# One projection unit per block with two products in the row tiles, q kept per block, and FFN units in the last head of a one-core attention kernel

## The chip, the core and the metric

The kernel runs on one core of one Trainium2 chip. The metric is the time of one execution in microseconds of device time. A profiled execution has a span a little under that time (1976.3 us against 1978.3 us before). Engines are called as in the profile: PE is TensorE's matmul side, PEld its weight loads, DVE VectorE, ACT ScalarE, POOL GpSimd, SP SyncE.

## The reference

Layer norm, then 32 heads of attention of 2048 queries on 2048 cached keys with head dimension 192, gated by the silu of a SwiGLU FFN of the same normed input:

```python
def reference(A_x, A_k_cache, A_v_cache, A_wq, A_wo, B_x, B_w1, B_w3, B_w2):
    xn = _layernorm(A_x)                                  # [1, 2048, 640]
    q = heads(xn @ A_wq)                                  # 32 heads of 192
    p = softmax(q @ k_cache^T * 192 ** -0.5)
    s = concat(p @ v_cache) @ A_wo
    h = silu(xn @ B_w1) * (xn @ B_w3)                     # F = 1536
    g = silu(h @ B_w2)
    return A_x + s * g
```

## The kernel before

Work goes in blocks: one head and 512 queries. A block has 8 units. A unit is six score matmuls, one exp on ACT of a 128x1024 tile in PSUM (the memory that matmuls write their sums to), and sixteen value matmuls that add into two PSUM tiles, called the output banks here (`obank`; each takes two of PSUM's eight banks). Scores run two units ahead of the values. Each matmul uses 64 of the 128 rows of the array, and a neighbour uses the other 64 at the same time (row tiles).

In the loop of head h, the q of head h+1 is projected as well. The two row tiles take the two halves of one contraction, so their results must be added: ACT copies one, DVE adds the other. A block of q needs this twice (`half` 1 and 0), and each time takes one of the two PSUM buffers `st2` that the scores also rotate through. The weight columns beside the last 64 of q carry a strip of the FFN (gate in even heads, up in odd heads).

```python
ps_st = ...tile_pool(name="ps_st", bufs=2, space=PSUM)      # [P, 1024] f32: two banks each

def project(h, qb, half):                                   # cut: head 0 has its own form
    qAB, qC = qtiles[h]
    qs = slice(qb * 512, (qb + 1) * 512)
    dst, w = qAB[:, half, qs], (L["wqB"] if half else L["wq"])
    ps = ps_st.tile([P, 1024], F32, tag="st2", name="ps")
    for c in range(DC):                                     # 5
        for r in range(2):
            rows = slice(r * 64, (r + 1) * 64)
            nc.tensor.matmul(ps[:, r * 512:(r + 1) * 512], lhsT=w[rows, c, 0:P],
                             rhs=xnT[rows, c, qs], start=(c == 0), stop=(c == DC - 1))   # L319
    part = hbp.tile([P, 512], F32, tag="part", name="part")
    nc.scalar.copy(out=part[:], in_=ps[:, 0:512])                                        # L322
    nc.vector.tensor_tensor(out=dst, in0=ps[:, 512:1024], in1=part[:], op=ALU.add)       # L323
    # then DMA copies of 64-row halves of qAB into qC

# values(n), when a block ends: the two output banks are evicted side by side
    nc.scalar.copy(out=osum[:], in_=ov[0])                                               # L405
    nc.vector.tensor_copy(out=opart[:], in_=ov[1])                                       # L406
    nc.vector.tensor_tensor(out=osum[:], in0=osum[:], in1=opart[:], op=ALU.add)          # L407

for n, (h, qb, p) in enumerate(stream):
    scores(n + 2)
    if h + 1 < H and p == (5 if h == 0 else 0):
        project(h + 1, qb, 1)
    if h + 1 < H and p == (NPAIR - 1 if h == 0 else NPAIR // 2):
        project(h + 1, qb, 0)
    values(n)
    if p == 0 and n > 0:
        finish_block(n - 1)
    if p == (6 if h == 0 else 2) and h < 2 * NPIG:
        swiglu(h, qb)                 # even heads: tanh on ACT, then DVE
    # cut: head 0's own projections, layer norm, loads
```

After the last head follow the FFN units that are left (`ps_gu`, full-row matmuls), the FFN's second product (`ps_f`) and the output product (`ps_s`).

## Time and profile before

| | before |
|---|---|
| median time | 1978.34 us (4 runs, 1977.82 to 1978.42) |
| span of the profile | 1976.3 us |
| PE / ACT / DVE busy | 1952.1 / 1319.6 / 738.3 us |
| a steady block (heads 1 to 30), mean | 12.81 us |

The first part of the profile's page (busy time and share of the span) and its part on the chain of work that ended last:

```profile
PE 1952.1 (99%) x27311; PEld 1386.0 (70%) x27311; DVE 738.3 (37%) x1109; ACT 1319.6 (67%) x1525; POOL 333.2 (17%) x570
...
PE 96%; ACT 2%; DVE 1%; DMA 1%; issue 0%; ACTq 0%
```

PE is the limit, and the page hides something. Matmuls are pipelined and their ends are modelled, so a PE that is 99% busy can still pause. The Trainium skill warns of this busy time too ("Trainium Kernel Development and Optimization", section "Performance Expectations": matmul busy time is a bad metric for how close a kernel is to its limit, because matmuls are pipelined). So I read distances from the start of one group of matmuls to the start of the next. In this trace six scores take 0.647 us, sixteen values 0.665 us, ten projection matmuls 1.076 us; these are the floors. Units of a block, from first score matmul to the next unit's first score matmul, mean over heads 1 to 30, computed from the starts in the trace:

| unit of the block | 0 | 1 | 2 | 3 | 4 | 5 | 6 | 7 | block |
|---|---|---|---|---|---|---|---|---|---|
| before, us | 1.314 | 1.324 | 2.432 | 1.314 | 1.314 | 1.314 | 2.483 | 1.314 | 12.81 |

Six units are within 0.012 us of their floor (0.647 + 0.665 = 1.312). Units 2 and 6 hold a half projection; 0.647 + 0.665 + 1.076 would be 2.388, so they lose 0.044 and 0.095 us. In even heads the second loss is larger. Lines of the timeline in an even head (start, duration, engine, line, operation; in brackets the engine's idle time and what ended it):

```profile
804.97 0.62 ACT L345 ACTIVATE pt<-qAB 64x512 bf16<-64x512 bf16 x1
...
805.49 1.00 ACT L369 ACTIVATE pT<-st 128x1024 bf16<-128x1024 f32 x1
...
806.19 0.38 PE L366 MATMUL st<-qC,KC 64*128 64x512 bf16 x1
...
806.21 0.38 PE L367 MATMUL st<-qC,KC 64*128 64x512 bf16 x1
806.55 1.26 PE L319 MATMUL ps<-xnT,wq 64*128 64x512 bf16 x10
...
806.68 1.02 ACT L369 ACTIVATE pT<-st 128x1024 bf16<-128x1024 f32 x1 [0.18 <-PE st L367]
```

The last pair of scores starts at 806.19 and would be followed after 0.215 us. The projection starts only at 806.55, 60 ns after the exp of L369 ends (805.49 + 1.00): it needs the PSUM buffer that this exp reads, and tanh (L345) had delayed the exp. The pause is 0.145 us here; in odd heads, which have no tanh, it is 0.038 us (both are the medians too).

The opening of a block in the last head, where no projection stands between the end of a block and the next values:

```profile
1643.11 0.96 DVE L406 COPY opart<-obank 128x772 f32<-128x772 f32 x1 [7.23 <-PE obank L395]
...
1643.33 0.38 PE L367 MATMUL st<-qC,KC 64*128 64x512 bf16 x1
1643.40 0.80 ACT L405 COPY osum<-obank 128x772 f32<-128x772 f32 x1
1644.09 1.04 ACT L369 ACTIVATE pT<-st 128x1024 bf16<-128x1024 f32 x1
1644.23 0.96 DVE L407 TENSOR_TENSOR osum<-osum,opart 128x772 f32<-128x772 f32 x1 [0.17 <-ACT osum L405]
1644.25 0.84 PE L395 MATMUL obank<-vt,pT 64*128 64x193 bf16 x16 [0.55 <-ACT osum L405]
```

PE waits 0.73 us with the values (to 1644.25, instead of 1643.52) until both output banks have been read.

### The profile page before, as it was taken

How to read it: one execution, taken by the hardware profiler on the slowest of the kernel's cores; microseconds unless marked ns; L12 is line 12 of the kernel's file. 1: busy time of each engine (PE TensorE's matmuls, PEld its weight loads, DVE VectorE, ACT ScalarE, POOL GpSimd, SP SyncE). 2: the span in 40 equal slices, each digit the busy share in tenths (PEclk: the TensorE clock that was granted, in tenths of full speed). 3: DMA queues.
4: the chain of work that ended last, by engine and by line, in shares of the span. 5: the costliest groups of instructions: out<-in, count | busy, mean ns of one | idle time of the engine just before them, and what ended most of it. 6: DMA issues, size and time to landing. Idle time of an engine off the chain costs nothing.

```text
span 1976.3 us, 60169 instructions
## 1 busy us (share of the span) xinstructions
PE 1952.1 (99%) x27311; PEld 1386.0 (70%) x27311; DVE 738.3 (37%) x1109; ACT 1319.6 (67%) x1525; POOL 333.2 (17%) x570
## 2 busy tenths in 40 slices
PE   7999999999999999999999999999999999999998
PEld 5677777777777777777777777777777776577776
DVE  5433434333344443334333333443433333521111
ACT  4677787777777777777777777777778777210000
POOL 2222112112221221122122112212211210000000
PEclk9999999999999999999999999999999999999999
DMA  6223233334333434363334343433323230928883
GB/s 153 56 56 91 62 100 66 95 67 100 69 98 69 101 69 99 69 167 67 100 69 101 67 101 69 87 80 73 91 58 92 62 80 4 263 37 150 151 143 70
DMA packets 359718, 177.96 MB, mean 90 GB/s; under 512 B 305552, under 2 KB 346256, under 8 KB 359456
## 3 DMA queue, kind: packets, MB, share of 16 engines
q1 hardware_dynamic: 331824, 113.92, 27.4%
q0 software_dynamic: 23120, 56.72, 11.6%
q8 instruction: 215, 3.52, 0.8%
q10 hardware_dynamic: 4512, 3.41, 0.6%
q14 instruction: 47, 0.39, 0.1%
HBM read 55.44 MB, written 27.79 MB: 42 GB/s over the span
## 4 chain that ended last, share of the span: by engine, by line
PE 96%; ACT 2%; DVE 1%; DMA 1%; issue 0%; ACTq 0%
PE obank L395 34%; PE st L366 30%; PE ps L319 14%; PE ps_s L106 11%; PE st L367 3%; PE ps_f L560 3%; PE ps_gu L531 1%; PE ps_gu L534 1%; ACT pT L369 1%; DMA vt<-in_A_k_cache_dram 1%; PE ps L312 0%; DVE stats L275 0%; ACT osum L405 0%; PE pst L291 0%; ACT xnT L294 0%
## 5 line engine op out<-in xcount | busy, mean ns | idle before, releaser
L369 ACT ACTIVATE pT<-st 128x1024 bf16<-128x1024 f32 x1024 | 1048.9, 1024 | 347.4 <-PE st L367 347.3
L395 PEld LDWEIGHTS <-pT 64*128 64x128 bf16 x16384 | 745.6, 94 | 215.0 <-issue 7.7
L395 PE MATMUL obank<-vt,pT 64*128 64x193 bf16 x16384 | 867.1, 243 | 5.2 <-ACT osum L405 2.9
L366 PE MATMUL st<-qAB,KA 64*128 64x512 bf16 x1024 | 385.1, 376 | 1.6 <-ACT pT L369 0.9
L366 PE MATMUL st<-qC,KC 64*128 64x512 bf16 x1024 | 385.0, 376 | 0.8 <-DVE KC L244 0.8
L366 PE MATMUL st<-qC,KB 64*128 64x512 bf16 x1024 | 385.0, 376 | 0.2 <-ACT qC L329 0.2
L367 PE MATMUL st<-qAB,KA 64*128 64x512 bf16 x1024 | 385.1, 376 | 0.0
L367 PE MATMUL st<-qC,KC 64*128 64x512 bf16 x1024 | 385.0, 376 | 0.0
L367 PE MATMUL st<-qAB,KB 64*128 64x512 bf16 x1024 | 385.0, 376 | 0.0
L332 POOL DMA_DIRECT2D qC<-qAB x254 | 134.4, 529 | 1250.3 <-DVE rl_all L413 654.8
L323 DVE TENSOR_TENSOR qAB<-ps,part 128x512 bf16<-128x512 f32 x248 | 171.4, 691 | 421.8 <-ACT part L322 420.9
L406 DVE COPY opart<-obank 128x772 f32<-128x772 f32 x128 | 123.0, 961 | 425.4 <-PE obank L395 425.4
L106 PE MATMUL ps_s<-wo_sb,oT 128*128 128x256 bf16 (+3 forms) x1536 | 208.8, 299 | 0.0
L106 PEld LDWEIGHTS <-oT 128*128 128x128 bf16 x1536 | 148.4, 98 | 60.4
L366 PEld LDWEIGHTS <-KC 64*128 64x128 bf16 x1024 | 96.2, 94 | 105.1 <-DVE KC L244 1.1
L319 PE MATMUL ps<-xnT,wq 64*128 64x512 bf16 x1240 | 155.7, 376 | 0.3
L319 PE MATMUL ps<-xnT,wqB 64*128 64x512 bf16 x1240 | 155.7, 376 | 0.2 <-ACT pT L369 0.2
L322 ACT COPY part<-ps 128x512 f32<-128x512 f32 x248 | 147.7, 596 | 10.7 <-PE ps L319 0.9
L407 DVE TENSOR_TENSOR osum<-osum,opart 128x772 f32<-128x772 f32 x128 | 123.2, 963 | 21.3 <-ACT osum L405 20.8
L414 DVE TENSOR_TENSOR ostage<-osum,rl_all 128x768 bf16<-128x768 f32 x128 | 122.6, 958 | 4.4
L319 PEld LDWEIGHTS <-wq 64*128 64x128 bf16 x1240 | 67.2, 94 | 77.6 <-issue 26.4
L319 PEld LDWEIGHTS <-wqB 64*128 64x128 bf16 x1240 | 67.2, 94 | 71.4 <-issue 20.0
(75 smaller groups left out, 1263.3 us busy)
## 6 DMA issues: line engine op xcount, KB each, us to landing
vt<-in_A_v_cache_dram SPq DMA_DIRECT2D x32, 768.0 KB, 6.6
o_scr<-ostage SPq DMA_DIRECT2D x16, 1536.0 KB, 8.9
qC<-qAB POOLq DMA_DIRECT2D x381, 64.0 KB, 1.9
wq<-in_A_wq_dram POOLq DMA_DIRECT2D x32, 240.0 KB, 3.5
wo_sb<-in_A_wo_dram POOLq DMA_DIRECT2D x1, 7680.0 KB, 38.5
KC<-KA POOLq DMA_DIRECT2D x31, 128.0 KB, 4.8
KC<-KB POOLq DMA_DIRECT2D x31, 128.0 KB, 5.9
x_all<-in_A_x_dram SPq DMA_DIRECT2D x4, 640.0 KB, 9.3
```

Of the source, the lines that this page charges most:

```text
L106: nc.tensor.matmul(ps[:, 0:w], lhsT=oT[:, k, :], rhs=wo_sb[:, k, c0:c1], start=(k == 0), stop=(k == OC - 1))
L319: nc.tensor.matmul(ps[:, r * 512:(r + 1) * 512], lhsT=w[rows, c, 0:P], rhs=xnT[rows, c, qs], start=(c == 0), stop=(c == DC - 1))
L322: nc.scalar.copy(out=part[:], in_=ps[:, 0:512])
L323: nc.vector.tensor_tensor(out=dst, in0=ps[:, 512:1024], in1=part[:], op=ALU.add)
L332: nc.gpsimd.dma_start(out=qC[0:64, half, qs], in_=qAB[64:P, half, qs])
L366: nc.tensor.matmul(st2[:, 0:512], lhsT=k0, rhs=q0, start=r == 0, stop=r == 2)
L367: nc.tensor.matmul(st2[:, 512:1024], lhsT=k1, rhs=q1, start=r == 0, stop=r == 2)
L369: nc.scalar.activation(out=pT2[:], in_=st2[:], func=ACT.Exp, scale=att_scale)
L395: nc.tensor.matmul(obanks[r][:, j * 256:j * 256 + DH + 1], lhsT=pT2[r * 64:(r + 1) * 64, t * 512 + j * P:t * 512 + (j + 1) * P], rhs=vt[r ...
L406: nc.vector.tensor_copy(out=opart[:], in_=ov[1])
L407: nc.vector.tensor_tensor(out=osum[:], in0=osum[:], in1=opart[:], op=ALU.add)
L414: nc.vector.tensor_tensor(out=ostage[:, qb * 4:qb * 4 + 4, hg * DH:(hg + 1) * DH], in0=osum[:, :, 0:DH], in1=rl.unsqueeze(2).to_broadcast( ...
```

## The change

Its intent: one PSUM buffer and one opening per block for the projection instead of two; no adding of halves, so less for ACT and DVE; and work for PE to cover the eviction of the output banks in the last head too. A second copy of xn^T with its 64-row halves swapped (`xnS`) lets each row tile run through the whole contraction of a product of its own: row tile 0 makes the first 128 columns of q, row tile 1 the FFN strip and the last 64. DVE casts one result, ACT the other. The output banks are now added without a copy in between.

```diff
-    qp = att.enter_context(tc.tile_pool(name="qp", bufs=2))        # q of a whole head
-    pp = att.enter_context(tc.tile_pool(name="pp", bufs=6))
+    qp = att.enter_context(tc.tile_pool(name="qp", bufs=5))        # q of a block
+    pp = att.enter_context(tc.tile_pool(name="pp", bufs=4))
+    xnS = xsp.tile([P, DC, SQ], BF16, name="xnS")
 ... (the weights of both products in one tile W, 64 rows each; loads)
+            nc.sync.dma_start(out=xnS[0:64, :, qs], in_=xnT[64:P, :, qs])
+            nc.sync.dma_start(out=xnS[64:P, :, qs], in_=xnT[0:64, :, qs])
 ... (project(h, qb, half) goes, except for head 0)
+    def two_products(W, qs):
+        ps = ps_st.tile([P, 1024], F32, tag="st2", name="ps")
+        for j in range(2 * DC):
+            for r in range(2):
+                rows = slice(r * 64, (r + 1) * 64)
+                xs = xnT if j % 2 == r else xnS
+                nc.tensor.matmul(ps[:, r * 512:(r + 1) * 512], lhsT=W[rows, j, :], rhs=xs[rows, j // 2, qs],
+                                 start=(j == 0), stop=(j == 2 * DC - 1))
+        return ps
+    def cast_pair(qAB, ps):
+        nc.vector.tensor_copy(out=qAB[:, 0, :], in_=ps[:, 0:512])
+        nc.scalar.copy(out=qAB[:, 1, :], in_=ps[:, 512:1024])
 ... (project(h, qb) = two_products, cast_pair, copies to qC; ffn_open / ffn_close: the same with
 ...  128 gate and 128 up columns, then tanh and the products)
-        opart = osp.tile([P, 4, DH + 1], F32, tag="opart", name="opart")
         nc.scalar.copy(out=osum[:], in_=ov[0])
-        nc.vector.tensor_copy(out=opart[:], in_=ov[1])
-        nc.vector.tensor_tensor(out=osum[:], in0=osum[:], in1=opart[:], op=ALU.add)
+        nc.vector.tensor_tensor(out=osum[:], in0=osum[:], in1=ov[1], op=ALU.add)
     for n, (h, qb, p) in enumerate(stream):
+        if p == 0 and n > 0:
+            if h + 1 < H:
+                project(h + 1, qb)
+            else:
+                ffn_open(qb)
         scores(n + 2)
-        if h + 1 < H and p == (5 if h == 0 else 0):
-            project(h + 1, qb, 1)
-        if h + 1 < H and p == (NPAIR - 1 if h == 0 else NPAIR // 2):
-            project(h + 1, qb, 0)
+        if h == 0 and qb == 0 and p == 5:
+            project(1, 0)
         values(n)
 ...
+        if p == 4 and h + 1 == H:
+            ffn_close(qb)
 ... (the tail makes three quarters of its ps_gu units)
```

More of the change, by code (lines that the diff above doesn't have):

```diff
@@ L162, in _kernel_impl @@
     FL = F - FPIG
+    FL2 = FL - P
+    assert FL2 > 0
     x2 = A_x[0]
@@ L180, in _kernel_impl @@
     fw = main.enter_context(tc.tile_pool(name="fw", bufs=1))
-    WX = max(NQT * D, FC * D + 2 * DC * FL)
+    WX = max(NQT * D, FC * D + 2 * DC * FL2)
     att = ExitStack()
@@ L185, in _kernel_impl @@
     vtp = att.enter_context(tc.tile_pool(name="vtp", bufs=1))
+    xsp = att.enter_context(tc.tile_pool(name="xsp", bufs=1))
     wqp = att.enter_context(tc.tile_pool(name="wqp", bufs=2))
-    qp = att.enter_context(tc.tile_pool(name="qp", bufs=2))
-    qlp = att.enter_context(tc.tile_pool(name="qlp", bufs=2))
-    pp = att.enter_context(tc.tile_pool(name="pp", bufs=6))
+    qp = att.enter_context(tc.tile_pool(name="qp", bufs=5))
+    qlp = att.enter_context(tc.tile_pool(name="qlp", bufs=5))
+    pp = att.enter_context(tc.tile_pool(name="pp", bufs=4))
     stp = att.enter_context(tc.tile_pool(name="stp", bufs=1))
@@ L205, in load_x, with gate_cols, load_w0, load_wf @@
                           in_=x2[g * 512:(g + 1) * 512, :].rearrange("(t p) d -> p t d", p=P))
+    def gate_cols(h):
+        wsel = B_w1 if h % 2 == 0 else B_w3
+        return wsel[:, (h // 2) * PGW:(h // 2 + 1) * PGW]
+    def load_w0():
+        W = wqp.tile([P, 2 * DC, P], BF16, tag="W", name="W")
+        nc.gpsimd.dma_start(out=W[:, 0:DC, :], in_=A_wq[:, 0:P].rearrange("(c p) d -> p c d", p=P))
+        nc.gpsimd.dma_start(out=W[:, DC:2 * DC, 0:PGW], in_=gate_cols(0).rearrange("(c p) f -> p c f", p=P))
+        nc.gpsimd.dma_start(out=W[:, DC:2 * DC, PGW:P], in_=A_wq[:, P:DH].rearrange("(c p) d -> p c d", p=P))
+        loads.setdefault(0, {}).update(W=W)
     def load_w(h):
-        wq = wqp.tile([P, DC, DH], BF16, tag="wq", name="wq")
-        nc.gpsimd.dma_start(out=wq[:], in_=A_wq[:, h * DH:(h + 1) * DH].rearrange("(c p) d -> p c d", p=P))
-        wqB = wqp.tile([P, DC, P], BF16, tag="wqB", name="wqB")
+        W = wqp.tile([P, 2 * DC, P], BF16, tag="W", name="W")
+        nc.gpsimd.dma_start(out=W[0:64, :, :], in_=A_wq[:, h * DH:h * DH + P].rearrange("(j p) d -> p j d", p=64))
         if h < 2 * NPIG:
-            wsel = B_w1 if h % 2 == 0 else B_w3
-            m = h // 2
-            nc.gpsimd.dma_start(out=wqB[:, :, 0:PGW], in_=wsel[:, m * PGW:(m + 1) * PGW].rearrange("(c p) f -> p c f", p=P))
-        else:
-            nc.gpsimd.memset(wqB[:, :, 0:PGW], 0.0)
-        nc.gpsimd.dma_start(out=wqB[:, :, PGW:P],
-                            in_=A_wq[:, h * DH + P:(h + 1) * DH].rearrange("(c p) d -> p c d", p=P))
-        loads.setdefault(h, {}).update(wq=wq, wqB=wqB)
+            nc.gpsimd.dma_start(out=W[64:P, :, 0:PGW], in_=gate_cols(h).rearrange("(j p) f -> p j f", p=64))
+        else:
+            nc.gpsimd.memset(W[64:P, :, 0:PGW], 0.0)
+        nc.gpsimd.dma_start(out=W[64:P, :, PGW:P],
+                            in_=A_wq[:, h * DH + P:(h + 1) * DH].rearrange("(j p) d -> p j d", p=64))
+        loads.setdefault(h, {}).update(W=W)
+    def load_wf():
+        W = wqp.tile([P, 2 * DC, P], BF16, tag="W", name="W")
+        for r, src in enumerate((B_w1, B_w3)):
+            nc.gpsimd.dma_start(out=W[r * 64:(r + 1) * 64, :, :],
+                                in_=src[:, FPIG:FPIG + P].rearrange("(j p) f -> p j f", p=64))
+        wrest["wf"] = W
     def load_k(h):
@@ L294, in ln_norm, with q_tiles @@
         copy(out=xnT[:, :, q0:q0 + 2 * P].rearrange("p c (k q) -> p k c q", k=2), in_=pst[:])
+        if i2 == 1:
+            qs = slice(g * 512, (g + 1) * 512)
+            nc.sync.dma_start(out=xnS[0:64, :, qs], in_=xnT[64:P, :, qs])
+            nc.sync.dma_start(out=xnS[64:P, :, qs], in_=xnT[0:64, :, qs])
     qtiles = {}
-    def project(h, qb, half):
-        L = loads[h]
-        if h not in qtiles:
-            qtiles[h] = (qp.tile([P, 2, SQ], BF16, tag="qAB", name="qAB"), qlp.tile([P, 2, SQ], BF16, tag="qC", name="qC"))
-        qAB, qC = qtiles[h]
+    def q_tiles(h, qb):
+        if (h, qb) not in qtiles:
+            qtiles[h, qb] = (qp.tile([P, 2, 512], BF16, tag="qAB", name="qAB"), qlp.tile([P, 2, 512], BF16, tag="qC", name="qC"))
+        return qtiles[h, qb]
@@ L306, in project, with move_q, project0 @@
+    def move_q(qAB, qC, half):
+        nc.gpsimd.dma_start(out=qC[0:64, half, :], in_=qAB[64:P, half, :])
+        if half == 0:
+            nc.gpsimd.dma_start(out=qC[64:P, 0, :], in_=qAB[0:64, 0, :])
+    def project0(qb, half):
+        W = loads[0]["W"]
+        qAB, qC = q_tiles(0, qb)
         qs = slice(qb * 512, (qb + 1) * 512)
-        dst = qAB[:, half, qs]
-        w = L["wqB"] if half else L["wq"]
         ps = ps_st.tile([P, 1024], F32, tag="st2", name="ps")
-        if h == 0:
-            for c in range(DC):
-                nc.tensor.matmul(ps[:, 0:512], lhsT=w[:, c, 0:P], rhs=xnT[:, c, qs], start=(c == 0), stop=(c == DC - 1))
-            copy = nc.scalar.copy if half else nc.vector.tensor_copy
-            copy(out=dst, in_=ps[:, 0:512])
-        else:
-            for c in range(DC):
-                for r in range(2):
-                    rows = slice(r * 64, (r + 1) * 64)
-                    nc.tensor.matmul(ps[:, r * 512:(r + 1) * 512], lhsT=w[rows, c, 0:P], rhs=xnT[rows, c, qs],
-                                     start=(c == 0), stop=(c == DC - 1))
-            part = hbp.tile([P, 512], F32, tag="part", name="part")
-            nc.scalar.copy(out=part[:], in_=ps[:, 0:512])
-            nc.vector.tensor_tensor(out=dst, in0=ps[:, 512:1024], in1=part[:], op=ALU.add)
@@ L325, in project @@
-        if h == 0 and qb == 0:
-            if half:
-                nc.vector.tensor_copy(out=qC[0:64, 1, qs], in_=ps[64:P, 0:512])
-            else:
-                nc.scalar.copy(out=qC[0:64, 0, qs], in_=ps[64:P, 0:512])
-                nc.vector.tensor_copy(out=qC[64:P, 0, qs], in_=ps[0:64, 0:512])
-        else:
-            nc.gpsimd.dma_start(out=qC[0:64, half, qs], in_=qAB[64:P, half, qs])
-            if half == 0:
-                nc.gpsimd.dma_start(out=qC[64:P, 0, qs], in_=qAB[0:64, 0, qs])
+        for c in range(DC):
+            nc.tensor.matmul(ps[:, 0:512], lhsT=W[:, half * DC + c, :], rhs=xnT[:, c, qs],
+                             start=(c == 0), stop=(c == DC - 1))
@@ new lines, in project0 @@
+        copy = nc.scalar.copy if half else nc.vector.tensor_copy
+        copy(out=qAB[:, half, :], in_=ps[:, 0:512])
+        if qb > 0:
+            move_q(qAB, qC, half)
+        elif half:
+            nc.vector.tensor_copy(out=qC[0:64, 1, :], in_=ps[64:P, 0:512])
+        else:
+            nc.scalar.copy(out=qC[0:64, 0, :], in_=ps[64:P, 0:512])
+            nc.vector.tensor_copy(out=qC[64:P, 0, :], in_=ps[0:64, 0:512])
+    def two_products(W, qs):
[7 more added lines that the diff above has]
+        return ps
@@ new lines, in cast_pair, with project, ffn_open @@
+    def cast_pair(qAB, ps):
+        nc.vector.tensor_copy(out=qAB[:, 0, :], in_=ps[:, 0:512])
+        nc.scalar.copy(out=qAB[:, 1, :], in_=ps[:, 512:1024])
+    def project(h, qb):
+        qAB, qC = q_tiles(h, qb)
+        cast_pair(qAB, two_products(loads[h]["W"], slice(qb * 512, (qb + 1) * 512)))
+        move_q(qAB, qC, 0)
+        move_q(qAB, qC, 1)
+    pairs = {}
+    def ffn_open(qb):
+        pairs[qb] = qp.tile([P, 2, 512], BF16, tag="qAB", name="qAB")
+        cast_pair(pairs[qb], two_products(wrest["wf"], slice(qb * 512, (qb + 1) * 512)))
@@ L336, in swiglu, with ffn_close @@
+    def ffn_close(qb):
+        z = pairs.pop(qb)
+        t = hbp.tile([P, 512], BF16, tag="pt", name="pt")
+        nc.scalar.activation(out=t[:], in_=z[:, 0, :], func=ACT.Tanh, scale=0.5)
+        nc.vector.scalar_tensor_tensor(out=t[:], in0=t[:], scalar=1.0, in1=z[:, 0, :], op0=ALU.add, op1=ALU.mult)
+        nc.vector.scalar_tensor_tensor(out=hT[:, FCP, qb * 512:(qb + 1) * 512], in0=t[:], scalar=0.5,
+                                       in1=z[:, 1, :], op0=ALU.mult, op1=ALU.mult)
     def swiglu(h, qb):
@@ L339, in swiglu @@
         qs = slice(qb * 512, (qb + 1) * 512)
-        z = qtiles[h][0][0:PGW, 1, qs]
+        z = qtiles[h, qb][0][0:PGW, 1, :]
         r0 = (m % 2) * PGW
@@ L343, in swiglu @@
         if h % 2 == 0:
-            t = hbp.tile([PGW, 512], BF16, tag="pt", name="pt")
-            nc.scalar.activation(out=t[:], in_=z, func=ACT.Tanh, scale=0.5)
-            nc.vector.scalar_tensor_tensor(out=hid, in0=t[:], scalar=1.0, in1=z, op0=ALU.add, op1=ALU.mult)
+            t = hbp.tile([P, 512], BF16, tag="pt", name="pt")
+            nc.scalar.activation(out=t[0:PGW, :], in_=z, func=ACT.Tanh, scale=0.5)
+            nc.vector.scalar_tensor_tensor(out=hid, in0=t[0:PGW, :], scalar=1.0, in1=z, op0=ALU.add, op1=ALU.mult)
         else:
@@ L356, in emit_scores @@
         KA, KB, KC = L["KA"], L["KB"], L["KC"]
-        qAB, qC = qtiles[h]
-        qs = slice(qb * 512, (qb + 1) * 512)
+        qAB, qC = qtiles[h, qb]
         lo = slice(p * P, (p + 1) * P)
@@ L361, in emit_scores @@
         st2 = ps_st.tile([P, 1024], F32, tag="st2", name="st2")
-        rounds = [(KA[0:64, lo], qAB[0:64, 0, qs], KA[64:P, hi], qAB[64:P, 0, qs]),
-                  (KB[0:64, lo], qC[0:64, 0, qs], KB[64:P, hi], qAB[64:P, 1, qs]),
-                  (KC[0:64, lo], qC[0:64, 1, qs], KC[64:P, lo], qC[64:P, 0, qs])]
+        rounds = [(KA[0:64, lo], qAB[0:64, 0, :], KA[64:P, hi], qAB[64:P, 0, :]),
+                  (KB[0:64, lo], qC[0:64, 0, :], KB[64:P, hi], qAB[64:P, 1, :]),
+                  (KC[0:64, lo], qC[0:64, 1, :], KC[64:P, lo], qC[64:P, 0, :])]
         for r, (k0, q0, k1, q1) in enumerate(rounds):
@@ L420, in loads_after @@
             load_w(h + 2)
+        if qb == NQB - 2 and h + 2 == H:
+            load_wf()
         if qb == 1 and h == H // 2:
@@ L424, in loads_after @@
             nc.sync.dma_start(out=wrest["w2"], in_=B_w2.rearrange("(c p) d -> p c d", p=P))
-            if FL > 0:
-                o1 = FC * D
-                for i, (nm, src) in enumerate((("w1", B_w1), ("w3", B_w3))):
-                    wrest[nm] = w_all[:, o1 + i * DC * FL:o1 + (i + 1) * DC * FL].rearrange("p (c f) -> p c f", f=FL)
-                    nc.sync.dma_start(out=wrest[nm], in_=src[:, FPIG:F].rearrange("(c p) f -> p c f", p=P))
+            o1 = FC * D
+            for i, (nm, src) in enumerate((("w1", B_w1), ("w3", B_w3))):
+                wrest[nm] = w_all[:, o1 + i * DC * FL2:o1 + (i + 1) * DC * FL2].rearrange("p (c f) -> p c f", f=FL2)
+                nc.sync.dma_start(out=wrest[nm], in_=src[:, F - FL2:F].rearrange("(c p) f -> p c f", p=P))
         if qb == NQB - 1:
@@ L451, in _kernel_impl @@
     nc.scalar.dma_start(out=vts[1][:, :, 0:DH], in_=A_k_cache[0, 0].rearrange("(t p) d -> p t d", p=P))
-    load_w(0)
+    load_w0()
     for i in range(4):
@@ L463, in _kernel_impl @@
     turn_over(12)
-    project(0, 0, 1)
-    project(0, 0, 0)
+    project0(0, 1)
+    project0(0, 0)
     copy_k(0)
@@ L499, in _kernel_impl @@
             if p == 3:
-                project(0, qb + 1, 1)
-                project(0, qb + 1, 0)
+                project0(qb + 1, 1)
+                project0(qb + 1, 0)
             if qb + 2 < NQB and 3 <= p < 7:
@@ L515, in _kernel_impl @@
     oTs = {}
-    w2_sb, w1_sb, w3_sb = wrest["w2"], wrest.get("w1"), wrest.get("w3")
+    w2_sb = wrest["w2"]
     def load_oT(i, pool):
@@ L527, in _kernel_impl @@
         qs = slice(qb * 512, (qb + 1) * 512)
-        for fl in range(FC - FCP):
-            ps = pools[(qb * (FC - FCP) + fl) % 2].tile([P, 1024], F32, tag="st2", name="ps_gu")
-            for c in range(DC):
-                nc.tensor.matmul(ps[:, 0:512], lhsT=w1_sb[:, c, fl * P:(fl + 1) * P], rhs=xnT[:, c, qs],
-                                 start=(c == 0), stop=(c == DC - 1))
-            for c in range(DC):
-                nc.tensor.matmul(ps[:, 512:1024], lhsT=w3_sb[:, c, fl * P:(fl + 1) * P], rhs=xnT[:, c, qs],
-                                 start=(c == 0), stop=(c == DC - 1))
+        for fl in range(FL2 // P):
+            ps = pools[(qb * (FL2 // P) + fl) % 2].tile([P, 1024], F32, tag="st2", name="ps_gu")
+            for r, w in enumerate((wrest["w1"], wrest["w3"])):
+                for c in range(DC):
+                    nc.tensor.matmul(ps[:, r * 512:(r + 1) * 512], lhsT=w[:, c, fl * P:(fl + 1) * P], rhs=xnT[:, c, qs],
+                                     start=(c == 0), stop=(c == DC - 1))
             t = fsb.tile([P, 512], BF16, tag="t", name="t")
@@ L539, in _kernel_impl @@
             nc.vector.scalar_tensor_tensor(out=a[:], in0=t[:], scalar=1.0, in1=ps[:, 0:512], op0=ALU.add, op1=ALU.mult)
-            nc.vector.scalar_tensor_tensor(out=hT[:, FCP + fl, qs], in0=a[:], scalar=0.5, in1=ps[:, 512:1024],
+            nc.vector.scalar_tensor_tensor(out=hT[:, FCP + 1 + fl, qs], in0=a[:], scalar=0.5, in1=ps[:, 512:1024],
                                            op0=ALU.mult, op1=ALU.mult)
```

## The prediction

> **What bounds it now.** TensorE. The profile's first part has PE busy 1952 of 1976 us (99%), ACT 67%, DVE 37%; the chain of waits is 96% PE; the granted clock is 0.998. All there is to win is time in which PE's matmul stream pauses. From start-to-start distances in the timeline:
>
> - pair of row-tile matmuls, 512 columns: 215 ns; six score matmuls 0.647 us; 16 value matmuls 0.665 us; a half projection (10 matmuls) 1.076 us. The Trainium skill, "TensorE: Matmul & The Clock Gate", section "Wait — 56ns, not 53.3ns?", gives N/2.4 GHz + about 2.5 ns (215.7 ns at N=512). The trace agrees: inside units PE runs at its stream rate.
> - floor of a steady block: 8 x 1.312 + 2.152 = 12.65 us. Measured: about 12.83.
>
> Excess over these floors, summed over the trace:
> - scores followed by a half projection, heads 1 to 30: 16.4 us. The projection needs a PSUM buffer that the exp of the unit before has only just left: 35 ns at the block's start, 145 ns in the middle where tanh (0.62 us) delayed that exp.
> - other steady transitions: 2.7 us.
> - head 0, opening of a block, where values wait for the output banks' eviction (ACT osum, DVE opart): about 4 us.
> - last head, the same wait (0.73 us x 4, no projection hides it): 2.2 us.
>
> **What the change does.**
> - PE work is the same: 2480 half-row matmuls for heads 1 to 31. FFN units put 4 x 20 of them (8.6 us) into the last head and take 4 x 10 full-row ones (8.6 us) out of the tail.
> - One PSUM buffer per block for the projection instead of two, taken at the opening, when the exp two units back has long ended. Its 2.15 us cover the eviction of the output banks.
> - ACT loses one of two copies (0.6 us) per block; DVE loses opart (0.96 us) and one of two adds (0.69 us). Neither is critical.
> - Output banks now come free in series: ACT copy, then DVE add. From the trace's times I estimate that this ends 2.3 us after the values; the next values come 2.8 us after. The casts should fit before the second next scores by about 0.3 us.
> - Head 0 gets eight half-swap transfers, issued about 7 us before use; 640 KB transfers land in under 10 us here, so a wait of a microsecond or two is possible.
> - Four pT buffers instead of six: about three are alive; no wait.
>
> **Critical share.** Of about 25 us of pauses I expect some 21 us to go: 16 from scores-to-projection waits, 3 from head 0, 2 from the last head; 1 to 4 us may return as small waits.
>
> **Predicted:** 1957 us, 8 in 10 between 1951 and 1967. Faster by over 2% 0.02, within 2% 0.95, slower by over 2% 0.03.
>
> **What would show it.** A steady block of 12.65 to 12.70 us; no pause before projections; PE matmul counts as before; PE's waits for osum in the last head gone; ACT busy about 70 us less, DVE about 200 us less; the ps_gu stage 8.6 us shorter.
>
> **What would make it wrong.** The serial eviction (ACT copy behind exp, then DVE add) may end later than 2.8 us and pause all 127 blocks (0.1 us each costs 12 us). The casts may hold their PSUM buffer past the second next scores. The half-swap transfers may queue behind head 1's K transposes. If switching between projection and scores costs something in itself, less is saved.

## The result

The changed kernel takes 1989.10 us (median of 4 runs, 1988.88 to 1989.26), the kernel before 1978.34 us. The ratio is 1.0055, 95% interval 1.0041 to 1.0069: slower by half a per cent, and within 2%. I had predicted 1957 us. (A ratio here is the mean time of one kernel's fast runs over that of the other's fast runs of the same rounds, so it is not quite the ratio of the medians quoted.)

| | before | after |
|---|---|---|
| span | 1976.3 | 1987.2 |
| PE / ACT / DVE busy, us | 1952.1 / 1319.6 / 738.3 | 1958.4 / 1260.5 / 530.7 |
| start to head 1 | 91.9 | 89.6 |
| heads 1 to 30 | 1537.1 | 1552.3 |
| last head, to the first ps_gu matmul | 46.4 | 53.3 |
| ps_gu units | 34.5 | 25.9 |
| rest | 266.3 | 266.1 |

The stages are cut at PE starts in the trace. Only the heads 1 to 30 got worse without getting more PE work: the last head's 6.9 us are the 8.6 us that left the ps_gu stage less 1.7 us saved. The same lines of the page:

```profile
PE 1958.4 (99%) x27351; PEld 1395.6 (70%) x27351; DVE 530.7 (27%) x861; ACT 1260.5 (63%) x1405; POOL 319.2 (16%) x572
...
PE 88%; DVE 5%; ACT 4%; issue 1%; DMA 1%; ACTq 0%; DVEq 0%
PE obank L446 30%; PE st L417 27%; PE ps L359 13%; PE ps_s L106 10%; DVE qAB L364 4%; ACT qAB L365 4%; PE st L418 3%; PE ps_f L612 3%; PE ps_gu L586 1%; DMA vt<-in_A_k_cache_dram 1%; PE ps L340 0%; ACT pT L420 0%; DVE stats L295 0%; PE pk L255 0%; PE pst L311 0%
```

PE's share of the chain fell from 96% to 88%, and two lines came in: the DVE cast L364 and the ACT cast L365, 4% each. The units of a block:

| unit of the block | 0 | 1 | 2 | 3 | 4 | 5 | 6 | 7 | block |
|---|---|---|---|---|---|---|---|---|---|
| before, us | 1.314 | 1.324 | 2.432 | 1.314 | 1.314 | 1.314 | 2.483 | 1.314 | 12.81 |
| after, us | 1.314 | 3.473 | 1.582 | 1.311 | 1.314 | 1.314 | 1.314 | 1.314 | 12.94 |

Unit 1 now holds the whole projection, 3.473 = 1.315 + 2.158, at its floor. The pauses in units 2 and 6 of before are gone: together 0.14 us per block. But unit 2, just behind the projection, takes 1.582 instead of 1.314 us. These 0.268 us, in 120 blocks, are 32 us. The timeline there (twenty projection matmuls end at 805.76; lines of the projection left out):

```profile
803.21 1.02 ACT L420 ACTIVATE pT<-st 128x1024 bf16<-128x1024 f32 x1 [0.28 <-PE st L418]
...
804.13 0.80 ACT L455 COPY osum<-obank 128x772 f32<-128x772 f32 x1
...
804.96 0.96 DVE L456 TENSOR_TENSOR osum<-osum,obank 128x772 f32<-128x772 f32 x1 [6.07 <-ACT osum L455]
...
805.76 0.38 PE L417 MATMUL st<-qAB,KA 64*128 64x512 bf16 x1
...
805.97 0.69 DVE L364 CAST qAB<-ps 128x512 bf16<-128x512 f32 x1
...
806.19 0.38 PE L417 MATMUL st<-qC,KC 64*128 64x512 bf16 x1
...
806.40 0.85 PE L446 MATMUL obank<-vt,pT 64*128 64x193 bf16 x16
...
806.70 0.58 ACT L365 CAST qAB<-ps 128x512 bf16<-128x512 f32 x1 [1.77 <-DVE qAB L364]
...
807.18 2.10 ACT L420 ACTIVATE pT<-st 128x1024 bf16<-128x1024 f32 x2
807.34 0.37 PE L417 MATMUL st<-qAB,KA 64*128 64x512 bf16 x1
```

The values start at 806.40, so the next scores should start at 807.07. They start at 807.34. They need the PSUM buffer that the projection wrote, and that is free when the second cast ends: 806.70 + 0.58 = 807.28. ACT's cast could have started beside DVE's at 805.97 (ACT's osum copy had ended at 804.93, its idle time is 1.77 us), but it starts only after DVE's has ended, 33 ns later in the median of the 128 pairs. The groups by line, and the waits (who waited for whom: us in all, times, longest), show that this is so every time:

```profile
L364 DVE CAST qAB<-ps 128x512 bf16<-128x512 f32 x128 | 88.5, 692 | 8.5 <-PE ps L359 1.4
...
L365 ACT CAST qAB<-ps 128x512 bf16<-128x512 f32 x128 | 74.9, 585 | 227.0 <-DVE qAB L364 223.5 <-issue 3.4
```

```profile
ACT qAB L365 <- DVE qAB L364: 223.5, 126, 1.9
...
PEld L418 <- issue: 35.5, 131, 0.8
...
PE st L417 <- ACT qAB L365: 1.0, 4, 0.3
```

And they show how well such a pause is hidden: PE's waiting for the second cast is given as 1.0 us in all, 4 times. By the groups, PE sits idle for 13.2 us in all before the first matmuls of L417 (1.6 us before the change), about 0.09 us in a block, where the distances show 0.27 us. Only the weight loads of L418 have 35.5 us of unexplained waiting, 131 times. In the built program ACT's cast waits on DVE's semaphore; in the trace 126 of the 128 wait for a semaphore that only DVE raises. The two casts write different halves of one SBUF tile and read different banks of one PSUM tile.

### The profile page after: what moved, and what is told of

Its sections match the earlier page's. It is cut to its first block, busy times and chain, and to the rows that moved or that the text cites. A ratio compares the mean times of both kernels' runs of the same rounds, so it can differ in the third digit from the quotient of the medians.

```text
span 1987.2 us, 60137 instructions
## 1 busy us (share of the span) xinstructions
PE 1958.4 (99%) x27351; PEld 1395.6 (70%) x27351; DVE 530.7 (27%) x861; ACT 1260.5 (63%) x1405; POOL 319.2 (16%) x572
## 4 chain that ended last, share of the span: by engine, by line
PE 88%; DVE 5%; ACT 4%; issue 1%; DMA 1%; ACTq 0%; DVEq 0%
PE obank L446 30%; PE st L417 27%; PE ps L359 13%; PE ps_s L106 10%; DVE qAB L364 4%; ACT qAB L365 4%; PE st L418 3%; PE ps_f L612 3%; PE ps_gu L586 1%; DMA vt<-in_A_k_cache_dram 1%; PE ps L340 0%; ACT pT L420 0%; DVE stats L295 0%; PE pk L255 0%; PE pst L311 0%
## 5 line engine op out<-in xcount | busy, mean ns | idle before, releaser
L417 PE MATMUL st<-qAB,KA 64*128 64x512 bf16 x1024 | 384.7, 376 | 13.2 <-ACT qAB L365 1.0
L418 PE MATMUL st<-qAB,KA 64*128 64x512 bf16 x1024 | 386.6, 378 | 0.0
L417 PE MATMUL st<-qC,KC 64*128 64x512 bf16 x1024 | 384.8, 376 | 0.8 <-DVE KC L264 0.8
L417 PE MATMUL st<-qC,KB 64*128 64x512 bf16 x1024 | 384.7, 376 | 0.8 <-DMA qC<-qAB 0.6
L418 PE MATMUL st<-qAB,KB 64*128 64x512 bf16 x1024 | 385.1, 376 | 0.0
L418 PE MATMUL st<-qC,KC 64*128 64x512 bf16 x1024 | 385.1, 376 | 0.0
L456 DVE TENSOR_TENSOR osum<-osum,obank 128x772 f32<-128x772 f32 x128 | 122.6, 958 | 945.8 <-ACT osum L455 945.8
L359 PE MATMUL ps<-xnT,W 64*128 64x512 bf16 x1280 | 299.5, 376 | 0.0
L359 PE MATMUL ps<-xnS,W 64*128 64x512 bf16 x1280 | 293.7, 376 | 0.0
L365 ACT CAST qAB<-ps 128x512 bf16<-128x512 f32 x128 | 74.9, 585 | 227.0 <-DVE qAB L364 223.5
L359 PEld LDWEIGHTS <-W 64*128 64x128 bf16 x2560 | 143.4, 94 | 103.4 <-issue 0.2
L417 PEld LDWEIGHTS <-KC 64*128 64x128 bf16 x1024 | 96.0, 94 | 105.0 <-DVE KC L264 1.1
L418 PEld LDWEIGHTS <-KA 64*128 64x128 bf16 x1024 | 96.1, 94 | 34.4 <-issue 33.9
L417 PEld LDWEIGHTS <-KA 64*128 64x128 bf16 x1024 | 96.3, 94 | 15.6 <-issue 1.3
L417 PEld LDWEIGHTS <-KB 64*128 64x128 bf16 x1024 | 96.1, 94 | 12.9
```

What stands on the lines that cost most here:

```text
L359: nc.tensor.matmul(ps[:, r * 512:(r + 1) * 512], lhsT=W[rows, j, :], rhs=xs[rows, j // 2, qs], start=(j == 0), stop=(j == 2 * DC - 1))
L365: nc.scalar.copy(out=qAB[:, 1, :], in_=ps[:, 512:1024])
L417: nc.tensor.matmul(st2[:, 0:512], lhsT=k0, rhs=q0, start=r == 0, stop=r == 2)
L418: nc.tensor.matmul(st2[:, 512:1024], lhsT=k1, rhs=q1, start=r == 0, stop=r == 2)
L456: nc.vector.tensor_tensor(out=osum[:], in0=osum[:], in1=ov[1], op=ALU.add)
```

## The experiments

All kernels gave correct results. Each was run in 3 rounds, beside the kernel before on the same chip: 1978.23 us for the first four, 1978.09 us for the next four, 1978.01 us for the last. "Changed" means the changed kernel at 1989.10 us. My theory: the two casts, one after the other, hold a PSUM buffer 0.27 us too long in each block. Rivals: the output banks, now freed by ACT and then DVE, come late; or a projection of twenty matmuls, or its second xn^T, costs PE time in itself.

| run | what differs | median, us | ratio to before (95%) | steady block, us |
|---|---|---|---|---|
| e1_act | changed, one ACT copy of both halves | 1955.52 | 0.9885 (0.9868 to 0.9901) | 12.67 |
| e2_dve | changed, one DVE copy of both halves | 1978.65 | 1.0001 (0.9985 to 1.0018) | 12.85 |
| e3_opart | changed, old eviction of the output banks | 1991.37 | 1.0066 (1.0049 to 1.0083) | 12.94 |
| e4_order | changed, projection behind the first scores | 1964.05 | 0.9927 (0.9911 to 0.9944) | 12.73 |
| e5_own | changed, halves of q in tiles of their own | 1988.71 | 1.0053 (1.0037 to 1.0070) | 12.94 |
| e8_swap | changed, ACT casts first | 1988.74 | 1.0053 (1.0037 to 1.0070) | 12.94 |
| e9_two | changed, both casts on ACT | 1958.32 | 0.9900 (0.9883 to 0.9916) | 12.70 |
| e7_ffn | e1_act, FFN units back in the tail | 1962.08 | 0.9919 (0.9902 to 0.9936) | 12.67 |
| e6_tanh | before, gate work later in the block | 1971.29 | 0.9967 (0.9950 to 0.9983) | 12.75 |

### e1_act

```diff
-        nc.vector.tensor_copy(out=qAB[:, 0, :], in_=ps[:, 0:512])
-        nc.scalar.copy(out=qAB[:, 1, :], in_=ps[:, 512:1024])
+        nc.scalar.copy(out=qAB[:], in_=ps[:].rearrange("p (k q) -> p k q", k=2))
```

> The changed kernel, with both halves of q evicted by one ACT copy of 128x1024 instead of a DVE cast followed by an ACT cast. Theory (serial casts hold the PSUM buffer that the second next scores need, 0.27 us in each of some 127 blocks): an ACT copy of 1024 columns takes about 1.00 us (estimate from 0.585 us at 512 and 0.797 us at 772 columns), so it ends about 1.27 us after the projection, inside the 1.31 us that scores and values take: the pause goes, 1952 to 1958 us. Rival (the output banks, freed by ACT and then DVE, come late; or the projection as one unit costs PE time in itself): nothing changes, 1986 to 1991 us.

Measured: 1955.52 us, 33.6 us less than the changed kernel. Nothing else was touched: order, matmuls, second xn^T and serial output banks are the same. Both rivals fall as explanations of the loss. The timeline behind the projection, as above:

```profile
815.97 0.38 PE L416 MATMUL st<-qAB,KA 64*128 64x512 bf16 x1
...
816.22 1.01 ACT L364 CAST qAB<-ps 128x1024 bf16<-128x1024 f32 x1 [1.05 <-PE ps L359]
...
816.62 0.88 PE L445 MATMUL obank<-vt,pT 64*128 64x193 bf16 x16
817.13 2.14 ACT L419 ACTIVATE pT<-st 128x1024 bf16<-128x1024 f32 x2
...
817.28 0.37 PE L416 MATMUL st<-qAB,KA 64*128 64x512 bf16 x1
```

The copy ends at 817.23; the scores start at 817.28, 0.66 us behind the values, which is their floor. It fits with almost nothing to spare, as the expectation had it. Unit 2 of the block is 1.318 us. This version is the fastest and beats both kernels.

### e2_dve

```diff
-        nc.vector.tensor_copy(out=qAB[:, 0, :], in_=ps[:, 0:512])
-        nc.scalar.copy(out=qAB[:, 1, :], in_=ps[:, 512:1024])
+        nc.vector.tensor_copy(out=qAB[:], in_=ps[:].rearrange("p (k q) -> p k q", k=2))
```

> The changed kernel, with both halves of q evicted by one DVE copy of 128x1024. Estimate 1.22 us (from 0.69 us at 512 and 0.96 us at 772 columns), so the buffer is free about 1.49 us after the projection: the theory expects a pause of about 0.18 us per block instead of 0.27, that is 1974 to 1982 us, between the changed kernel and the one with the ACT copy. Rival (output banks or projection in itself): 1986 to 1991 us.

Measured: 1978.65 us, inside the range.

```profile
L364 DVE CAST qAB<-ps 128x1024 bf16<-128x1024 f32 x128 | 156.8, 1225 | 8.4 <-PE ps L359 1.4
```

The DVE copy of 128x1024 takes 1.225 us, and unit 2 of the block 1.497 us: a pause of 0.18 us. So the time follows the length of the hold: 1.01 us (e1) gives no pause, 1.225 us gives 0.18, the pair of casts with its hand-over (1.31 us from first start to last end) gives 0.27.

### e3_opart

```diff
+        opart = osp.tile([P, 4, DH + 1], F32, tag="opart", name="opart")
         nc.scalar.copy(out=osum[:], in_=ov[0])
-        nc.vector.tensor_tensor(out=osum[:], in0=osum[:], in1=ov[1], op=ALU.add)
+        nc.vector.tensor_copy(out=opart[:], in_=ov[1])
+        nc.vector.tensor_tensor(out=osum[:], in0=osum[:], in1=opart[:], op=ALU.add)
```

> The changed kernel with the old eviction of the output banks put back (ACT copy and DVE copy side by side, then the add). Theory: the values after the projection don't wait for these banks, nothing changes, 1987 to 1991 us. Rival (serial eviction of the output banks costs the time): 1955 to 1970 us.

Measured: 1991.37 us, 0.4 us above the range that I gave the theory, and nowhere near the rival's. Heads 1 to 30 take 1552.3 us as in the changed kernel. The stretch before head 1 takes 2.0 us more (91.6 against 89.6): the trace has pauses of 1.6 and 1.7 us at openings of its blocks, where the changed kernel has 0.5 and 0.6; the trace shows why in the first: DVE, which also makes the layer norm there, has one instruction of 0.96 us more to do before its cast, which starts at 47.33 instead of 46.14 us, and the scores follow ACT's cast by 0.06 us as before. In heads 1 to 30, behind a projection, the serial eviction of the output banks costs nothing.

### e4_order

```diff
+        scores(n + 2)
         if p == 0 and n > 0:
             ...
-        scores(n + 2)
```

> The changed kernel with the projection put behind the first scores of the block, as the kernel before had it. Theory: between the projection and the next use of its PSUM buffer there are then values, scores and values, about 1.98 us, so that serial casts of 1.53 us fit; what comes back is the short wait for the exp before the projection, 0.04 us per block: 1955 to 1963 us. Rival (one unit of twenty matmuls, or the second xn^T, costs PE time in itself): 1983 us or more.

Measured: 1964.05 us, 1 us above the range, far below the rival's. The slow serial casts are still there, and unit 3 is at 1.314 us: with one more group of values before the buffer is needed, they fit. Units 2, with scores, projection and values, are 3.507 us in the median, 0.034 above the 3.473 us of the projection's unit in the changed kernel: the short wait for the exp, as expected. What I had not expected are 28 of 120 blocks at about 3.59 us and five more between 3.61 and 3.93. The trace tells where the 28 lose it: in all 120 blocks the projection starts 51 ns after the end of the exp that it waits for. In the 28 the two row tiles of the scores run 0.10 us apart, where they run 0.02 us apart in the 87 blocks near 3.51 us; so that exp, which needs both, and the projection behind it come 0.08 us later. Why the row tiles drift apart stays open, and so do most of the five.

### e5_own and e8_swap

e5_own gives each half of q an SBUF tile of its own (`qA` and `qB` in place of `qAB[:, 0]` and `qAB[:, 1]`, everywhere). e8_swap exchanges the two lines of `cast_pair`.

> The changed kernel with the two halves of q in SBUF tiles of their own. The ACT cast waits for the DVE cast in the changed kernel; this asks which shared tile makes it wait. If it is the shared q tile, the wait goes, the casts run side by side and the time falls to about 1956 us. If it is the shared PSUM tile (which I now think, because the built program still has the wait), the time stays at 1987 to 1991 us and ACT's cast still starts right after DVE's.

> The changed kernel with the order of the two casts reversed: ACT takes its half first, DVE waits. Theory (the sum of the two casts and one handing over holds the buffer): the sum stays, 1986 to 1991 us, with the wait now on DVE's side. Rival (not the buffer, but the exp behind ACT's late cast holds PE): the exp starts 0.5 us earlier and the pause goes, 1955 to 1965 us.

Measured: 1988.71 and 1988.74 us, as the theory expected in both. The casts in e8_swap, where the wait has moved to DVE:

```profile
L365 DVE CAST qAB<-ps 128x512 bf16<-128x512 f32 x128 | 88.6, 692 | 88.1 <-ACT qAB L364 88.1
...
L364 ACT CAST qAB<-ps 128x512 bf16<-128x512 f32 x128 | 74.9, 585 | 135.0 <-PE ps L359 135.0
```

In e5_own ACT's cast still waits for DVE's:

```profile
ACT qB L368 <- DVE qA L367: 223.7, 126, 1.9
```

The two casts then share nothing but the PSUM tile `ps`. So it is the shared PSUM tile that puts them in order, although they read different banks of it; this is by exclusion. A version with a PSUM tile for each half was not tried: all eight banks are in use, and the scores' tile would have to be split too. So it is not shown that the two casts would then run side by side. That the hardware itself allows the two reads is stated by the Trainium skill ("PSUM — Partial Sum Buffer", section "Specifications (TRN2)": ScalarE and VectorE can access PSUM in parallel as long as they don't collide in a bank), and the trace before agrees, for two tiles: the 0.80 and 0.96 us copies that were shown running at once. e8_swap also shows that it does not matter whether ACT's next exp is delayed: there ACT casts first and that exp starts 0.50 us earlier in the block, and the time is the same.

### e9_two

```diff
-        nc.vector.tensor_copy(out=qAB[:, 0, :], in_=ps[:, 0:512])
+        nc.scalar.copy(out=qAB[:, 0, :], in_=ps[:, 0:512])
         nc.scalar.copy(out=qAB[:, 1, :], in_=ps[:, 512:1024])
```

> The changed kernel with two casts of 512 columns as before, but both on ACT. Theory: back to back on one engine they take about 1.10 us (0.585 each, overlapping by some 0.08 as neighbouring ACT instructions do in the trace), against 1.32 us across two engines and 1.01 us in one instruction, so that the pause is 0 to 0.05 us per block: 1955 to 1963 us. Rival (two instructions cost it, wherever they run): 1980 us or more.

Measured: 1958.32 us. Two instructions in themselves are not the trouble. Unit 2 is 1.341 us, so a pause of 0.03 us per block is left.

```profile
L365 ACT CAST qAB<-ps 128x512 bf16<-128x512 f32 x128 | 75.7, 591 | 0.0
L364 ACT CAST qAB<-ps 128x512 bf16<-128x512 f32 x128 | 75.0, 586 | 133.9 <-PE ps L359 133.9
```

From first start to last end, the two casts take 1.07 us on ACT (the second starts 0.10 us before the first ends) and 1.31 us across the engines. Of the 0.24 us between them, 0.14 us are the crossing, a gap of 0.03 us in place of that overlap, and 0.10 us come of DVE's cast being the slower one (0.69 us). In the changed kernel, e1_act, e2_dve, e5_own, e8_swap and e9_two alike, the next scores start 51 to 53 ns after the end of the last cast (medians of 120 blocks). The Trainium skill advises ("Perfetto Trace Analysis", section "Optimizing Scalar/DVE Operations") that where these engines aren't saturated but cause bubbles on others, breaking up instructions may let work complete sooner. Here the opposite held: broken up over two engines the work took 1.31 us, over two ACT instructions 1.07 us, in one ACT instruction 1.01 us.

### e7_ffn

The diff takes the FFN units out of the last head of e1_act (no `ffn_open`, `ffn_close`, `load_wf`; `FL2 = FL`, so that the tail makes all ps_gu units as before).

> The version with one ACT copy (1955.5 us), with the FFN units put back from the last head into the tail. If FFN units in the last head are worth what the trace of before says (0.73 us of waiting for the output banks at each of four block openings, and nothing else): 1957 to 1959.5 us. If they are worth nothing: 1955.5 us.

Measured: 1962.08 us; FFN units in the last head are worth 6.6 us, where I expected at most 4. Last head and ps_gu stage together take 50.3 + 34.5 us, against 52.3 + 25.9 in e1_act. The opening of a block of the last head without a projection:

```profile
1648.83 0.80 ACT L454 COPY osum<-obank 128x772 f32<-128x772 f32 x1
...
1649.66 0.96 DVE L455 TENSOR_TENSOR osum<-osum,obank 128x772 f32<-128x772 f32 x1 [9.33 <-ACT osum L454]
1649.68 0.24 PE L445 MATMUL obank<-vt,pT 64*128 64x193 bf16 x1 [0.55 <-ACT osum L454]
...
1650.67 0.51 PE L445 MATMUL obank<-vt,pT 64*128 64x193 bf16 x8 [0.75 <-DVE osum L455]
```

I had taken the 0.73 us of before for the cost of an uncovered eviction. But the serial eviction takes longer: PE waits for ACT's copy (0.55 us of idle time) and then for DVE's add (0.75 us), and a block of this head takes 12.21 us instead of the 10.51 us of eight units: 1.69 us each, four times. So the serial eviction does cost something, where no projection covers it.

### e6_tanh

```diff
-        if p == (6 if h == 0 else 2) and h < 2 * NPIG:
+        if p == (6 if h == 0 else 4) and h < 2 * NPIG:
             swiglu(h, qb)
```

> The kernel before with one thing changed: in heads 1 to 30 the FFN's gate work (tanh and its products) is done two units later in the block, behind the second half projection. The prediction said that tanh delays the exp that this half projection waits for, 145 ns instead of 38 in every even head. If so, 60 blocks lose 0.107 us each, 6.4 us: 1970.5 to 1973.5 us. If the 145 ns have another cause: 1977.5 to 1979 us.

Measured: 1971.29 us, ratio 0.9967. This is the kernel before with one number changed. Unit 6 of its block falls from 2.483 to 2.426 us, and even heads now take the 50.96 us of odd heads instead of 51.39 (medians). So the pause in the middle of an even head's block was tanh delaying the exp whose buffer the projection needs, as the prediction had read it.

## Why the prediction was wrong

The step that failed is one sentence: "The casts should fit before the second next scores by about 0.3 us." The text gives only this result; the sum behind it was, after the projection's end, 0.21 us until a cast starts, 0.69 us for the longer cast, and 0.06 us until PE goes on, 0.96 us in all, against the 1.31 us that scores and values take. That took the two casts to run side by side, since they are on two engines and in two banks. The runs showed them one after the other: 0.217 + 0.692 + 0.033 + 0.585 + 0.052 = 1.579 us (medians), a pause of 0.27 us per block, 124 times in heads 1 to 31, 33 us. The order was in the built program, which I had before me: ACT's cast waits on DVE's semaphore. I had read the order of instructions there but not their waits. I had named the risk ("The casts may hold their PSUM buffer past the second next scores"), but with no number to it, and my range stopped at 1967 us.

The other terms, one by one:

- Pauses between scores and projection, "16.4 us", to go. They went: e1_act, which has no cast pause, takes 16.3 us less than before in heads 1 to 30 (1520.8 against 1537.1). e6_tanh confirms the cause of the larger part on the kernel before.
- "The serial eviction ... may end later than 2.8 us": it did not; DVE's add ended at 805.92, and the values behind the projection came at 806.40. e3_opart confirms that undoing it gains nothing.
- Last head, 2 us (four waits of 0.73 us are 2.9 us, not the 2.2 us of the prediction): 1.7 us in the changed kernel, 2.7 us in e1_act. The reason was right, but e7_ffn shows that I did not see the other side: with the new eviction, leaving the last head uncovered would have cost 1.69 us per block and not 0.73.
- Head 0, 3 us: 2.3 us, and 3.2 us in e1_act. The half-swap transfers made PE wait nowhere: the waits list no PE wait for them, and the units of head 0 that hold a projection take 3.47 us there too, except the first (3.50 us).
- Steady block of 12.65 to 12.70 us: 12.94 in the changed kernel, 12.67 in e1_act.
- ACT about 70 us less: 59. DVE about 200 us less: 208. ps_gu 8.6 us shorter: 8.6.
- That switching between projection and scores costs something in itself: it does not; unit 1 of the block is at its floor.

So the gains were about right in sum (e1_act, at 1955.5 us, is close to the 1957 us where I had put the changed kernel), and one term, put at nothing, was 33 us.

## What to carry to other kernels

When a tile's eviction is split over two engines to make it faster, look in the built program, or in the trace's waits, whether the second engine waits for the first: two engines that read one PSUM tile may be put in order even where they read different banks, and then the split can be slower than one instruction on one engine (here 1.31 us against 1.01 us on ACT and 1.225 us on DVE). When two users rotate through two PSUM buffers, write down for each how long the buffer is held and how much other work stands before its next use; here 0.27 us decided whether a change gained 23 us or lost 11. A pause that recurs in every block need not show as idle time of a pipelined engine; compare the distances between starts with the floor of the same group.

## What the Trainium skill lacked or had wrong

- "PSUM — Partial Sum Buffer" says that ScalarE and VectorE can access PSUM in parallel as long as there is no bank collision. No page says that a built program may still put in order two engines' reads of different banks of one PSUM tile. Here ACT's cast waited for DVE's in 126 of 128 pairs of casts (33 ns from one's end to the other's start in the median; 0.27 us of pause in each block).
- "TensorE: Matmul & The Clock Gate", Part 3, gives about 4 ns between the starts of matmuls in different row tiles. Here partners start about 20 ns apart in most of the traces before and after (806.19 and 806.21 above), about 57 ns apart in most of e1_act's, and 0.10 us apart in the scores of 28 blocks of e4_order. Near to the page's figure are the first two matmuls of a projection there: 5 to 6 ns in 90 of 120 blocks. The distance from pair to pair stays 215 to 216 ns.
- "Perfetto Trace Analysis", section "Optimizing Scalar/DVE Operations", advises breaking up instructions where they cause bubbles on another engine. It lacks the case in which the parts are put in order because they share a source tile: 1.31 us in two parts on two engines, 1.01 us in one on ACT.
